# Holding seven output tiles on chip in an attention kernel, for one K slot less

## The chip, the cores and the metric

One Trainium2 chip, one core. The time is that of one launch in device microseconds; of several runs the median is taken.

## The reference

Two independent attention blocks A and B, with the same shapes and their own tensors; their outputs stand side by side in the result. Softmax is over 512 keys, everything in bfloat16.

```python
B, Sq, D = 16, 64, 640;  H, Sk, Dh = 32, 512, 128
q = (x @ wq).reshape(B, Sq, H, Dh).transpose(0, 2, 1, 3)
scores = einsum("bhqd,bhkd->bhqk", q, k_cache) * Dh ** -0.5
o = einsum("bhqk,bhkd->bhqd", softmax(scores), v_cache)
y = o.transpose(0, 2, 1, 3).reshape(B, Sq, H * Dh) @ wo
out = concatenate([y_A, y_B], axis=-1)          # 16 x 64 x 1280
```

## The kernel before

**Packs, groups, phases.** The work is cut into 128 *packs*. A pack is two batches (128 rows of queries) by four heads; it needs 1 MB of K and 1 MB of V. Four packs make a *group* (one pair of batches, 16 heads); groups are numbered 0 to 31. Eight groups make a *phase*: phase 0 is block A with heads 0 to 15, phase 1 block A with heads 16 to 31, phases 2 and 3 the same for block B. The output projection of a group is summed over its four packs in PSUM. In phases 0 and 2 the sum goes to `acc` in SBUF; in phases 1 and 3 it is added to `acc`, and the finished tile of 128 x 640 (160 KB) is stored. So there are sixteen results: groups 8 to 15 (block A) and 24 to 31 (block B). The first is stored at 230.6 us, the last at 710.7 us and, in two halves, at the end.

**What a pack does on each engine.** The names are the operations of the plan; each has an `em_` function.
- SyncE (SP) issues the loads `LDK` and `LDV`, per group `LDX` (queries), per phase `LDWQ` and `LDWO` (weights), and the stores `ST`, and `STH` for the two halves of the last result.
- TensorE: `QP` (query projection), `S` and `SL` (scores), `TR` (transposes of the probabilities), `PV` (probabilities times V), `OP` (output projection).
- VectorE (DVE): `KT` (transposes K from `kn_ring` into `kt_ring`), `RC` (reciprocals of row sums), `TE` (transposed probabilities from PSUM to `pT_sb`), `OS` (the sum of projections into `acc` or the result).
- ScalarE (ACT): `QE`, `EX` (exponential, with row sums), `OE` (product from PSUM to `oT_sb`, in two halves), `ZO` (zeros PSUM).
- GpSimd (POOL): `NM` (probabilities times reciprocal), `WP` (weights rearranged), `XS` and `XC` (transposed queries, kept in `xs_sb` for the second half of the heads).

**Order.** Nothing is scheduled at run time. `build_plan` gives each operation a due time in units of packs (pack n's scores are at time n; `AT` holds the offsets) and sorts each engine's program by it. SP's program is sorted by times of its own (`loads`): in steady state V of pack n stands at n - 2.1, K of pack m at m - 4.6, and a result's store 2.8 packs behind the start of its group's last pack. Every operation lists the resources that it reads and writes; the waits are worked out from those. Where the plan does not count an operation for the engine that has to wait, `stand_in` puts a later or equivalent operation in its place: SP's loads of K wait for `SL` of the pack that used the slot, loads of V for `TR` of the pack after it, a store for an `RC` behind its `OS`. All loads and stores go through SP's one queue, in program order.

**Buffers.** `kn_ring` has NK = 6 slots of 1 MB (8 KB in each partition), `v_ring` NV = 4. `out_sb` is one result tile, used by all stores in turn. `xs_sb` has one slot of 1280 bytes in a partition for each of the eight pairs of batches, the size of a result; its last reader in a block is `XC` of the group whose result is then formed.

**The end.** The last two packs, 126 and 127, are *narrow*: their products use row groups of 64 and their V comes in two DMAs, one for each batch. For pack 126 the operations `TE` and `PV` still take both batches at once, into banks 4 to 7; its projection goes in two halves (`OPH`) between the steps of pack 127. Pack 127 goes by halves throughout (`TRH`, `TEH` and `TEX`, `PVH`, `OEH`, `OPH`, `OSH`, `STH`). Beside it a test of all row sums runs: `FL1` on VectorE, `FLM` (a 1 x 1 matmul) on TensorE between the two `OPH` of pack 127, and `FLC`, which writes a flag. Every engine reads the flag at the end, and goes through a second, general plan only where a row sum is out of bounds; it doesn't with these inputs. TensorE runs packs 0 to 127 in a loop of four packs; what follows the `OP` of pack 125 stands behind the loop.

Of the kernel before, what the change touches and what calls it, by code (L numbers as in the profile page):

```python
# [20 lines left out]
class Cfg:  # L21
    NK = 6
    NV = 4
# [9 lines left out]
    KSPLIT = 8  # L33
    NARROW = 2
    AFTER = 24
    AT = dict(XT=-2.585, XE=-2.383, XS=-1.65, XC=-0.788, QP=-0.428, QE=-0.224, KT=(-0.672, -0.39), SL=0.1, S=0,
# [3 lines left out]
              TRH=(1.0, 1.05), TEH=(1.15, 1.2), TEX=1.2, PVH=(1.45, 1.46), OEH=(1.5, 1.55), OPY=(1.1, 1.57),  # L40
              OPZ=(1.65, 1.7), OSH=(1.75, 1.8), STH=(1.85, 1.9), FL1=1.3, FLM=1.68, FLC=1.82, WP0=(-1.6, -1.59, -0.7, -0.69, 0.25, 0.26, 1.25, 1.26),
              WP1=(-3.5, -2.55, -2.45, -1.5, -0.5, 0.5, 0.6, 1.5))
# [44 lines left out]
def build_plan(dims, cfg, general):  # L87
# [18 lines left out]
    def add_output(n):  # L106
        g, j = n // NJ, n % NJ
        final = n >= 0 and dims["FINAL"](g // NBP)
        apart = 0 <= n < cfg.KSPLIT or n >= N - cfg.NARROW
        for b in range(0 if apart else 1, 2):  # L110
            tv = n + AT["PV"]
            op = add("sp", "LDV", (n, b), tv - 0.3, [],
                     [("v" if n >= 0 else "absent", n % cfg.NV, i) for i in ((b,) if apart else (0, 1))])
            loads.append((n - cfg.NV + AT["PV"] + 0.2 if n >= 0 else -99.0, 3, op))
        if n == N - 1:
            for a in range(2):
                add("pe", "TRH", a, n + AT["TRH"][a], [("pn", n % cfg.NPN, i) for i in (2 * a, 2 * a + 1)] + [("ident",)],
                    [("SB", 2), ("SB", 3)] if a == 0 else [("SB", 0), ("SB", 1)])
                add("pe", "PVH", a, n + AT["PVH"][a], [("pT", 0, a), ("pT", 1, a)] + [("v", n % cfg.NV, b) for b in range(2)],
                    [("B", 4), ("B", 5)] if a == 0 else [("SB", 2), ("SB", 3)])  # L120
                add("act", "OEH", (n, a), n + AT["OEH"][a], [],
                    [("B", 4), ("B", 5), ("xe", 0)] if a == 0 else [("SB", 2), ("SB", 3), ("xe", 1)])
                add("pe", "OPH", (n, a), n + AT["OPZ"][a], [("xe", 0), ("xe", 1), ("wo", j)], [("B", 6 + a)])
                add("dve", "OSH", (g, a), n + AT["OSH"][a], [("acc", g % NBP)], [("B", 6 + a), ("out_sb", a)])
                loads.append((n + AT["STH"][a], 5,
                              add("sp", "STH", (g, a), n + AT["STH"][a], [("out_sb", a)], [("out_dram", g, a)])))
            add("dve", "TEH", 0, n + AT["TEH"][0], [], [("SB", 2), ("SB", 3), ("pT", 0, 0), ("pT", 1, 0)])
            add("dve", "TEH", 1, n + AT["TEH"][1], [], [("SB", 0), ("pT", 0, 1)])
            add("act", "TEX", 0, n + AT["TEX"], [], [("SB", 1), ("pT", 1, 1)])
            return  # L130
        if n > -2:
            add("pe", "TR", n, n + AT["TR"], [("pn", n % cfg.NPN, i) for i in range(4)] + [("ident",)],
                [("B", 4), ("B", 5)])
        add("dve", "TE", n, n + AT["TE"], [], [("B", 4), ("B", 5)] + [("pT", b, a) for b in range(2) for a in range(2)])
        add("pe", "PV", n, n + AT["PV"], [("pT", b, a) for b in range(2) for a in range(2)] + [("v", n % cfg.NV, 0), ("v", n % cfg.NV, 1)],
            [("B", 4), ("B", 5), ("B", 6), ("B", 7)])
        add("act", "OE", (n, 0), n + AT["OE"][0], [], [("B", 4), ("B", 5), ("oT", 0)])
        if n == N - 2:
            add("act", "OEH", (n, 1), n + AT["OE"][1], [], [("B", 6), ("B", 7), ("oT", 1)])
            for s in range(2):  # L140
                add("pe", "OPH", (n, s), n + 1 + AT["OPY"][s], [("oT", 0), ("oT", 1), ("wo", j)], [("B", 6 + s)])
            return
        add("act", "OE", (n, 1), n + AT["OE"][1], [], [("B", 6), ("B", 7), ("oT", 1)])
        add("act", "ZO", n, n + AT["ZO"], [("zeros",)], [("B", 6), ("B", 7)])
        add("pe", "OP", n, n + AT["OP"], [("oT", 0), ("oT", 1), ("wo", j)], [("B", 6), ("B", 7)])
        if j == NJ - 1:
            bp = g % NBP
            add("dve", "OS", g, n + AT["OS"], [("acc", bp)], [("B", 6), ("B", 7)]
                + ([("out_sb", 0), ("out_sb", 1)] if final else [("acc", bp)]))
            if final:  # L150
                loads.append((n + AT["ST"], 5, add("sp", "ST", g, n + AT["ST"], [("out_sb", s) for s in range(2)], [("out_dram", g)])))

    if not general:
        add("pool", "INIT1", 0, -10.0, [], [("out_sb", s) for s in range(2)])
        add("pool", "INIT2", 0, -9.9, [("out_sb", s) for s in range(2)], [("ident",)])
    for g in range(N // NJ + 1):
# [7 lines left out]
        if first:  # L164
            add("pool", "XS", g, n0 + AT["XS"], [("xe", 0), ("xe", 1)], [("xs", g % NBP)])
            if g:
                loads.append((txt - 4.05, 0, add("sp", "LDX", g, txt - 0.5, [], [("xn", g % cfg.NXN)])))
            else:
                add("act", "LDX", g, -21.0, [], [("xn", g % cfg.NXN)])
        add("pool", "XC", g, n0 + AT["XC"], [("xe", 0), ("xe", 1)] if first else [("xs", g % NBP)], [("xT", g % cfg.NX)])  # L170
    for ph in range(NPH):
# [93 lines left out]

    own = {"XC", "QE", "KT", "NM", "TE", "OE", "ZO", "OS", "LDV"}

# [13 lines left out]
    def stand_in(d, op):  # L281
# [29 lines left out]
        if d.kind == "OS":  # L311
            return at[("PV", d.idx * NJ + NJ)]
        if d.kind == "TE":
            return at[("PV", d.idx)]
# [190 lines left out]
def mha_kernel(nc, blocks, out, cfg=None):  # L505
# [26 lines left out]
    with contextlib.ExitStack() as es:  # L532
# [19 lines left out]
        zeros = sb("zeros", [128, 1], BF16)  # L552
        out_sb = sb("out_sb", [128, D], BF16)
        acc = sb("acc", [128, NBP, D], F32)
# [20 lines left out]
        def pack_info(n):  # L575
            g, j = n // NJ, n % NJ
            ph = g // NBP
            return ph // NSUB, g % NBP, j, ph % NSUB * HPH + 4 * j

        def em_INIT1(e, op):  # L580
            ins = e.memset(out_sb[:, 0:128], 1.0)
            return ins, ins

        def em_INIT2(e, op):
            ins = e.affine_select(ident[:, :], out_sb[:, 0:128], [[1, 128]], ALU.is_equal, 0.0, base=0,
                                  channel_multiplier=-1)
            return ins, ins
# [254 lines left out]
        def em_OSH(e, op):  # L842
            g, s = op.idx
            cols = slice(s * NH0, (s + 1) * NH0)
            ins = e.tensor_tensor(out_sb[:, cols], acc[:, g % NBP, cols], out_ps[:, s, :], ALU.add)
            return ins, ins

        def em_STH(e, op):
            (g, s), blk, bp = op.idx, op.idx[0] // NBP // NSUB, op.idx[0] % NBP
            cols = slice(s * NH0, (s + 1) * NH0)  # L850
            dst = out[2 * bp:2 * bp + 2, :, blk * D:(blk + 1) * D].rearrange("b q n -> (b q) n")
            ins = e.dma_start(dst[:, cols], out_sb[:, cols])
            return ins, ins

        def em_TE(e, op):
            dst = pT_sb[:, :].rearrange("p b t q -> p (b t q)")
            if op.idx == -2:
                ins = e.memset(dst, 0.0)
                return ins, ins
            ins = e.tensor_copy(dst, ps[:, 4:6, :].rearrange("p b c -> p (b c)").bitcast(BF16))  # L860
            return ins, ins

        def em_PV(e, op):
            n = op.idx
            tall, tiles, per = (32, 4, 16) if wide(n) else (64, 2, 8)
            first = last = None
            for a in range(4 // tiles):
                for b in range(2):
                    for t in range(per):
                        for s in range(tiles):  # L870
                            rows = slice(tall * s, tall * s + tall)
                            i, c = a * tiles + s, a * per + t
                            last = e.matmul(ps[:, 4 + i, 64 * b:64 * b + 64], v_ring[rows, n % NV, b, c, :],  # L873
                                            pT_sb[rows, b, c, :], start=(t == 0 and i < 2), stop=(t == per - 1),
# [4 lines left out]
        def em_OE(e, op):  # L879
            a = op.idx[1]  # L880
            ins = e.activation(oT_sb[:, 2 * a:2 * a + 2, :], o_ps[:, 2 * a:2 * a + 2, :], ACTF.Copy)  # L881
            return ins, ins
# [15 lines left out]
        def em_OS(e, op):  # L898
# [5 lines left out]
            else:  # L904
                dst = out_sb[:, :].rearrange("p (s c) -> p s c", s=2) if sub == NSUB - 1 else part
                ins = e.tensor_tensor(dst, part, out_ps, ALU.add)
            return ins, ins

        def em_ST(e, op):
            blk, bp = op.idx // NBP // NSUB, op.idx % NBP  # L910
            dst = out[2 * bp:2 * bp + 2, :, blk * D:(blk + 1) * D].rearrange("b q n -> (b q) n")
            ins = e.dma_start(dst, out_sb[:, :])
            return ins, ins
# [163 lines left out]
```

## Time and profile before

| | |
|---|---|
| time, median of 3 runs | 731.28 us (731.04 to 732.07) |
| the profiled execution: time, span | 730.47 us, 728.7 us |
| mean granted TensorE clock | 0.991 |
| busy: TensorE, VectorE, ScalarE, GpSimd | 92%, 70%, 73%, 57% of the span |
| moved by DMA | 295.02 MB, 405 GB/s over the span |
| of that written | 2.62 MB |

The span runs from the first to the last recorded instruction; the execution's time has a little around it. In a row of the timeline the first number is the start in us, the second the duration; in the chain of waits a piece named "DMA" runs from a transfer's issue to its landing, and "issue" is time in which an engine waited for nothing that the profile shows. L873 is line 873 of the listing above.

### The profile page before, as it was taken

The page shows a single profiled execution, that of the slowest core. Times are in us where ns is not written, and L with a number is a line of the kernel's source. Part 1 is how long each engine was busy: PE and PEld are TensorE (multiplying, and loading weights), DVE is VectorE, ACT ScalarE, POOL GpSimd, SP SyncE. Part 2 cuts the span into 40 slices and gives each one's busy share as a digit, 9 for nine tenths or more (in the row PEclk, how much of TensorE's full clock was granted, in tenths as well). Part 3 has the DMA queues.
Part 4 walks back from the last instruction along what each step waited for, and adds up shares of the span by engine and source line. Part 5 has one row for each costly group of instructions (what it writes and reads, how often), then busy time and mean ns, then how long its engine had stood idle before and what let it go on. Part 6 is the DMA issues. An engine that isn't in the chain of part 4 may idle for free.

```text
span 728.7 us, 61194 instructions
## 1 busy us (share of the span) xinstructions
PE 673.8 (92%) x28502; PEld 528.6 (73%) x28502; DVE 513.5 (70%) x690; ACT 533.0 (73%) x1574; POOL 417.5 (57%) x596
## 2 busy tenths in 40 slices
PE   2779999999999999999997899999999789999998
PEld 1457878778777777777776677777777568787775
DVE  6347777777777776776775667676777577778776
ACT  1448887878877777777776677767778677878785
POOL 4535656566875455554883555465587445555652
PEclk9889999999999999999999999999999999999999
DMA  8999999999999999999999999999999999999994
GB/s 338 400 406 414 414 416 413 414 416 415 412 402 411 418 416 415 417 415 417 415 410 399 417 413 413 415 413 414 415 416 405 405 415 418 416 417 418 416 416 158
DMA packets 72336, 295.02 MB, mean 405 GB/s; under 512 B 7664, under 2 KB 20080, under 8 KB 55920
## 3 DMA queue, kind: packets, MB, share of 16 engines
q1 hardware_dynamic: 72160, 294.52, 100.3%
q8 instruction: 10, 0.16, 0.1%
q10 hardware_dynamic: 144, 0.16, 0.1%
q14 instruction: 22, 0.18, 0.1%
HBM read 292.03 MB, written 2.62 MB: 404 GB/s over the span
## 4 chain that ended last, share of the span: by engine, by line
PE 54%; DMA 27%; SPq 8%; POOL 4%; DVE 3%; issue 2%; ACT 1%; DVEq 0%
PE ps L873 13%; PE ps L893 12%; DMA kn_ring<-in_B_k_cache_dram 12%; PE ps L688 11%; PE ps L718 10%; DMA kn_ring<-in_A_k_cache_dram 7%; PE ps L780 7%; DMA v_ring<-in_B_v_cache_dram 5%; SPq L631 4%; POOL pn_ring L768 3%; DMA v_ring<-in_A_v_cache_dram 3%; SPq L615 2%; DVE pT_sb L860 1%; DMA ws_sb<-in_A_wq_dram 1%; DVE kt_ring L703 1%
## 5 line engine op out<-in xcount | busy, mean ns | idle before, releaser
L768 POOL TENSOR_SCALAR pn_ring<-pn_ring,recip 128x512 bf16<-128x512 bf16 x508 | 343.0, 694 | 255.3 <-DVE recip L760 254.6
L703 DVE STREAM_TRANSPOSE kt_ring<-kn_ring 128x1024 f32<-128x1024 f32 x256 | 311.9, 1230 | 117.9 <-DMA kn_ring<-in_B_k_cache_dram 79.7
L747 ACT ACTIVATE pn_ring<-ps 128x512 bf16<-128x512 f32 x512 | 296.4, 592 | 6.3 <-PE ps L718 6.3
L860 DVE COPY pT_sb<-ps 128x2048 bf16<-128x2048 bf16 x128 | 154.2, 1205 | 48.1 <-PE ps L780 47.6
L873 PE MATMUL ps<-pT_sb,v_ring 32*128 32x64 bf16 x16448 | 160.7, 192 | 19.6 <-DMA v_ring<-in_B_v_cache_dram 8.2
L688 PE MATMUL ps<-xT_ring,wqp_sb 128*128 128x128 bf16 x2560 | 165.8, 220 | 11.2 <-POOL xT_ring L677 11.2
L873 PEld LDWEIGHTS ps<-pT_sb,v_ring 32*128 32x128 bf16 x16448 | 145.7, 91 | 34.3 <-DMA v_ring<-in_B_v_cache_dram 15.2
L688 PEld LDWEIGHTS ps<-xT_ring,wqp_sb 128*128 128x128 bf16 x2560 | 157.5, 114 | 17.5 <-issue 11.5
L893 PE MATMUL ps<-wo_sb,oT_sb 128*128 128x320 bf16 x1024 | 163.1, 303 | 0.0
L881 ACT ACTIVATE oT_sb<-ps 128x256 bf16<-128x256 f32 x257 | 84.7, 381 | 104.4 <-PE ps L873 104.4
L718 PE MATMUL ps<-kt_ring,qs_ring 32*64 32x512 bf16 x4096 | 139.1, 381 | 4.5 <-issue 4.5
L694 ACT ACTIVATE qs_ring<-ps 128x512 bf16<-128x512 f32 x128 | 76.4, 597 | 71.2 <-PE ps L688 68.9
L780 PEld LDWEIGHTS ps<-ident,pn_ring 64*128 64x128 bf16 x4096 | 68.4, 95 | 68.0 <-ACT oT_sb L881 43.4
L893 PEld LDWEIGHTS ps<-wo_sb,oT_sb 128*128 128x128 bf16 x1024 | 90.3, 98 | 36.7
L747 ACT ACTIVATION_READ_ACCUMULATOR pn_ring<-ps 128x1 f32 x512 | 105.3, 206 | 0.0
L780 PE MATMUL ps<-ident,pn_ring 64*128 64x64 bf16 x4096 | 83.0, 191 | 13.5 <-POOL pn_ring L768 7.5
L718 PEld LDWEIGHTS ps<-kt_ring,qs_ring 32*64 32x64 bf16 x4096 | 53.0, 103 | 33.3 <-issue 5.7
L760 DVE RECIPROCAL recip<-rowsum 128x2 f32<-128x2 f32 x256 | 38.4, 156 | 42.2 <-ACT pn_ring L747 40.6
L885 ACT ACTIVATE ps<-zeros 128x256 f32<-128x256 bf16 x128 | 49.5, 387 | 4.1
L656 POOL COPY wqp_sb<-ws_sb 128x1280 bf16<-128x1280 bf16 x32 | 39.6, 1255 | 9.2 <-DMA ws_sb<-in_A_wq_dram 6.5
L668 ACT ACTIVATE xe_sb<-ps 128x640 bf16<-128x640 bf16 x32 | 23.0, 717 | 3.2 <-PE ps L662 3.1
L677 POOL COPY xT_ring<-xe_sb 128x640 bf16<-128x640 bf16 x16 | 11.5, 718 | 16.7 <-PE ps L780 16.7
(42 smaller groups left out, 103.3 us busy)
## 6 DMA issues: line engine op xcount, KB each, us to landing
kn_ring<-in_B_k_cache_dram SPq DMA_DIRECT2D x128, 512.0 KB, 16.5
v_ring<-in_B_v_cache_dram SPq DMA_DIRECT2D x62, 1024.0 KB, 16.8
kn_ring<-in_A_k_cache_dram SPq DMA_DIRECT2D x112, 512.0 KB, 13.2
v_ring<-in_A_v_cache_dram SPq DMA_DIRECT2D x56, 1024.0 KB, 14.6
kn_ring<-in_A_k_cache_dram SPq DMA_DIRECT2D x32, 256.0 KB, 9.8
v_ring<-in_A_v_cache_dram SPq DMA_DIRECT2D x16, 512.0 KB, 10.4
ws_sb<-in_A_wq_dram SPq DMA_DIRECT2D x10, 512.0 KB, 9.6
wo_sb<-in_A_wo_dram SPq DMA_DIRECT2D x8, 640.0 KB, 12.7
```

Of the source, the lines that this page charges most:

```text
L688: last = e.matmul(ps[:, 1, f * 128:(f + 1) * 128], w[:, kt, f, :], xT_ring[:, xs, kt, :], start=(kt == 0), stop=(kt == KT - 1))
L694: ins = e.activation(qs_ring[:, op.idx % NQ].rearrange("p f b q -> p (f b q)"), ps[:, 1, :], ACTF.Copy, scale=scale)
L703: ins = e.transpose(dst.rearrange("p t b (h l) -> p t h b l", h=8, l=2), src)
L718: last = e.matmul(ps[64 * b:64 * b + 64, i, :], qs_ring[rows, n % NQ, f, b, :], kt_ring[rows, n % NKT, :, f // 2, b, :, f % 2], start=(f = ...
L747: ins = e.activation(dst, src, ACTF.Exp, scale=1.0, accum_out=sum_of(h))
L768: ins = e.tensor_scalar(pn_view(h), pn_view(h), recip[:, h:h + 1], 1.0, ALU.mult, ALU.mult)
L780: last = e.transpose(pt_bank(b)[:, 64 * c:64 * c + 64], pn[rows, c, :], ident[rows, rows], tile_position=(64 * b, 0))
L860: ins = e.tensor_copy(dst, ps[:, 4:6, :].rearrange("p b c -> p (b c)").bitcast(BF16))
L873: last = e.matmul(ps[:, 4 + i, 64 * b:64 * b + 64], v_ring[rows, n % NV, b, c, :], pT_sb[rows, b, c, :], start=(t == 0 and i < 2), stop=(t ...
L881: ins = e.activation(oT_sb[:, 2 * a:2 * a + 2, :], o_ps[:, 2 * a:2 * a + 2, :], ACTF.Copy)
L885: ins = e.activation(z_ps, zeros[:, :].unsqueeze(2).broadcast_to([128, 2, 128]), ACTF.Copy)
L893: last = e.matmul(out_ps[:, s, :], oT_sb[:, i, :], wo_sb[:, 4 * j + i, s * NH0:(s + 1) * NH0], start=(j == 0 and i == 0), stop=(j == NJ - ...
```

## The change

- **Results.** `out_sb` becomes seven tiles (NHOLD = 7). The results of groups 8 to 14 stay in them. The other results, group 15 and all of block B, are written into the `xs_sb` slot of their pair of batches.
- **Stores.** The stores of groups 8 to 14, and those of groups 24 and 25 (LATE), move in SP's program to 125.95, behind the last V (at 124.9) and the store of group 30 (at 125.8), ahead of the two `STH`.
- **K ring.** NK goes from 6 to 5: 8 KB in each partition less, for 7.5 KB more of `out_sb`.
- **Pack 126.** `TE` and `PV` go by batches: `TE` and `PV` for the first, the new `TEB` and `PVB` for the second. The first two of the four products go to banks 0 and 1, columns 256 to 383, where the last scores stood, and `OE` takes them from there. The transposes `TRH` 1 of pack 127 write other columns of these banks, and by the plan's resources wait for that `OE`.
- **Flag.** `FLM` moves from 1.68 to 1.72, behind the second `OPH` of pack 127 (1.7).

```diff
-    NK = 6
+    NK = 5
...
+    NHOLD = 7
+    LATE = (24, 25)
+    LATEST = -2.05
...
-              ... FL1=1.3, FLM=1.68, FLC=1.82, ...
+              ... FL1=1.3, FLM=1.72, FLC=1.82, ...
...
+        held = g < N // NJ // 2 and g % NBP < cfg.NHOLD
+        result = [("held", g % NBP, s) if held else ("xs", g % NBP, s) for s in range(2)]
...
+        if n == N - 2:
+            for b in range(2):
+                add("dve", ("TE", "TEB")[b], n, n + AT["TE"] + 0.01 * b, [], [("B", 4 + b), ("pT", b, 0), ("pT", b, 1)])
+                add("pe", ("PV", "PVB")[b], n, n + AT["PV"] + 0.01 * b, [("pT", b, 0), ("pT", b, 1), ("v", n % cfg.NV, b)],
+                    [("SB", 0), ("SB", 1), ("B", 6), ("B", 7)])
+            add("act", "OE", (n, 0), n + AT["OE"][0], [], [("SB", 0), ("SB", 1), ("oT", 0)])
+            add("act", "OEH", (n, 1), n + AT["OE"][1], [], [("B", 6), ("B", 7), ("oT", 1)])
...
             if final:
-                loads.append((n + AT["ST"], 5, add("sp", "ST", g, n + AT["ST"], [("out_sb", s) for s in range(2)], [("out_dram", g)])))
+                late = held or g in cfg.LATE
+                loads.append((N + cfg.LATEST + 0.001 * g if late else n + AT["ST"], 5,
+                              add("sp", "ST", g, N + cfg.LATEST + 0.001 * g if late else n + AT["ST"], result, [("out_dram", g)])))
...
-        out_sb = sb("out_sb", [128, D], BF16)
+        out_sb = sb("out_sb", [128, cfg.NHOLD, D], BF16)
...
+        def result(g):
+            if g // NBP < NSUB and g % NBP < cfg.NHOLD:
+                return out_sb[:, g % NBP]
+            return xs_sb[:, g % NBP, 0:D]
...
         def em_TE(e, op):
             dst = pT_sb[:, :].rearrange("p b t q -> p (b t q)")
+            if op.idx == NPACK - 2:
+                ins = e.tensor_copy(pT_sb[:, 0].rearrange("p t q -> p (t q)"), pt_bank(0))
+                return ins, ins
...
+        def o_bank(n, i):
+            return ps[:, i, 256:384] if n == NPACK - 2 and i < 2 else ps[:, 4 + i, 0:128]
...
         def em_ST(e, op):
...
-            ins = e.dma_start(dst, out_sb[:, :])
+            ins = e.dma_start(dst, result(op.idx))
```

More of the change, by code (lines that the diff above doesn't have):

```diff
@@ L40 @@
               TRH=(1.0, 1.05), TEH=(1.15, 1.2), TEX=1.2, PVH=(1.45, 1.46), OEH=(1.5, 1.55), OPY=(1.1, 1.57),
-              OPZ=(1.65, 1.7), OSH=(1.75, 1.8), STH=(1.85, 1.9), FL1=1.3, FLM=1.68, FLC=1.82, WP0=(-1.6, -1.59, -0.7, -0.69, 0.25, 0.26, 1.25, 1.26),
+              OPZ=(1.65, 1.7), OSH=(1.75, 1.8), STH=(1.85, 1.9), FL1=1.3, FLM=1.72, FLC=1.82, WP0=(-1.6, -1.59, -0.7, -0.69, 0.25, 0.26, 1.25, 1.26),
               WP1=(-3.5, -2.55, -2.45, -1.5, -0.5, 0.5, 0.6, 1.5))
@@ L123, in add_output @@
                 add("pe", "OPH", (n, a), n + AT["OPZ"][a], [("xe", 0), ("xe", 1), ("wo", j)], [("B", 6 + a)])
-                add("dve", "OSH", (g, a), n + AT["OSH"][a], [("acc", g % NBP)], [("B", 6 + a), ("out_sb", a)])
+                add("dve", "OSH", (g, a), n + AT["OSH"][a], [("acc", g % NBP)], [("B", 6 + a), result[a]])
                 loads.append((n + AT["STH"][a], 5,
-                              add("sp", "STH", (g, a), n + AT["STH"][a], [("out_sb", a)], [("out_dram", g, a)])))
+                              add("sp", "STH", (g, a), n + AT["STH"][a], [result[a]], [("out_dram", g, a)])))
             add("dve", "TEH", 0, n + AT["TEH"][0], [], [("SB", 2), ("SB", 3), ("pT", 0, 0), ("pT", 1, 0)])
@@ L133, in add_output @@
                 [("B", 4), ("B", 5)])
+        if n == N - 2:
[5 more added lines that the diff above has]
+            add("act", "OEH", (n, 1), n + AT["OE"][1], [], [("B", 6), ("B", 7), ("oT", 1)])
+            for s in range(2):
+                add("pe", "OPH", (n, s), n + 1 + AT["OPY"][s], [("oT", 0), ("oT", 1), ("wo", j)], [("B", 6 + s)])
+            return
         add("dve", "TE", n, n + AT["TE"], [], [("B", 4), ("B", 5)] + [("pT", b, a) for b in range(2) for a in range(2)])
@@ L137, in add_output @@
         add("act", "OE", (n, 0), n + AT["OE"][0], [], [("B", 4), ("B", 5), ("oT", 0)])
[L138 to L142, printed above, removed]
         add("act", "OE", (n, 1), n + AT["OE"][1], [], [("B", 6), ("B", 7), ("oT", 1)])
@@ L148, in add_output @@
             add("dve", "OS", g, n + AT["OS"], [("acc", bp)], [("B", 6), ("B", 7)]
-                + ([("out_sb", 0), ("out_sb", 1)] if final else [("acc", bp)]))
+                + (result if final else [("acc", bp)]))
             if final:
-                loads.append((n + AT["ST"], 5, add("sp", "ST", g, n + AT["ST"], [("out_sb", s) for s in range(2)], [("out_dram", g)])))
+                late = held or g in cfg.LATE
+                loads.append((N + cfg.LATEST + 0.001 * g if late else n + AT["ST"], 5,
+                              add("sp", "ST", g, N + cfg.LATEST + 0.001 * g if late else n + AT["ST"], result, [("out_dram", g)])))
     if not general:
-        add("pool", "INIT1", 0, -10.0, [], [("out_sb", s) for s in range(2)])
-        add("pool", "INIT2", 0, -9.9, [("out_sb", s) for s in range(2)], [("ident",)])
+        add("pool", "INIT1", 0, -10.0, [], [("held", 0, s) for s in range(2)])
+        add("pool", "INIT2", 0, -9.9, [("held", 0, s) for s in range(2)], [("ident",)])
     for g in range(N // NJ + 1):
@@ L164, in build_plan @@
         if first:
-            add("pool", "XS", g, n0 + AT["XS"], [("xe", 0), ("xe", 1)], [("xs", g % NBP)])
+            add("pool", "XS", g, n0 + AT["XS"], [("xe", 0), ("xe", 1)], [("xs", g % NBP, s) for s in range(2)])
             if g:
@@ L169, in build_plan @@
                 add("act", "LDX", g, -21.0, [], [("xn", g % cfg.NXN)])
-        add("pool", "XC", g, n0 + AT["XC"], [("xe", 0), ("xe", 1)] if first else [("xs", g % NBP)], [("xT", g % cfg.NX)])
+        add("pool", "XC", g, n0 + AT["XC"], [("xe", 0), ("xe", 1)] if first else [("xs", g % NBP, s) for s in range(2)], [("xT", g % cfg.NX)])
     for ph in range(NPH):
@@ L264, in build_plan @@
             op.deps = [d for d in op.deps if d.kind != "WP"]
-    own = {"XC", "QE", "KT", "NM", "TE", "OE", "ZO", "OS", "LDV"}
+    own = {"XC", "QE", "KT", "NM", "TE", "TEB", "OE", "ZO", "OS", "LDV"}
     def for_pe(d):
@@ L312, in stand_in @@
             return at[("PV", d.idx * NJ + NJ)]
+        if d.kind == "TEB":
+            return at[("PVB", d.idx)]
         if d.kind == "TE":
@@ L578, in pack_info @@
             return ph // NSUB, g % NBP, j, ph % NSUB * HPH + 4 * j
+        def result(g):
+            if g // NBP < NSUB and g % NBP < cfg.NHOLD:
+                return out_sb[:, g % NBP]
+            return xs_sb[:, g % NBP, 0:D]
         def em_INIT1(e, op):
-            ins = e.memset(out_sb[:, 0:128], 1.0)
+            ins = e.memset(out_sb[:, 0, 0:128], 1.0)
             return ins, ins
         def em_INIT2(e, op):
-            ins = e.affine_select(ident[:, :], out_sb[:, 0:128], [[1, 128]], ALU.is_equal, 0.0, base=0,
+            ins = e.affine_select(ident[:, :], out_sb[:, 0, 0:128], [[1, 128]], ALU.is_equal, 0.0, base=0,
                                   channel_multiplier=-1)
@@ L844, in em_OSH @@
             cols = slice(s * NH0, (s + 1) * NH0)
-            ins = e.tensor_tensor(out_sb[:, cols], acc[:, g % NBP, cols], out_ps[:, s, :], ALU.add)
+            ins = e.tensor_tensor(result(g)[:, cols], acc[:, g % NBP, cols], out_ps[:, s, :], ALU.add)
             return ins, ins
@@ L851, in em_STH @@
             dst = out[2 * bp:2 * bp + 2, :, blk * D:(blk + 1) * D].rearrange("b q n -> (b q) n")
-            ins = e.dma_start(dst[:, cols], out_sb[:, cols])
+            ins = e.dma_start(dst[:, cols], result(g)[:, cols])
             return ins, ins
@@ L861, in em_TE, with em_TEB, em_PVB, product @@
             return ins, ins
+        def em_TEB(e, op):
+            ins = e.tensor_copy(pT_sb[:, 1].rearrange("p t q -> p (t q)"), pt_bank(1))
+            return ins, ins
         def em_PV(e, op):
-            n = op.idx
+            return product(e, op.idx, (0,) if op.idx == NPACK - 2 else (0, 1))
+        def em_PVB(e, op):
+            return product(e, op.idx, (1,))
+        def o_bank(n, i):
+            return ps[:, i, 256:384] if n == NPACK - 2 and i < 2 else ps[:, 4 + i, 0:128]
+        def product(e, n, halves):
             tall, tiles, per = (32, 4, 16) if wide(n) else (64, 2, 8)
@@ L867, in em_PV @@
             for a in range(4 // tiles):
-                for b in range(2):
+                for b in halves:
                     for t in range(per):
@@ L872, in em_PV @@
                             i, c = a * tiles + s, a * per + t
-                            last = e.matmul(ps[:, 4 + i, 64 * b:64 * b + 64], v_ring[rows, n % NV, b, c, :],
+                            last = e.matmul(o_bank(n, i)[:, 64 * b:64 * b + 64], v_ring[rows, n % NV, b, c, :],
                                             pT_sb[rows, b, c, :], start=(t == 0 and i < 2), stop=(t == per - 1),
@@ L880, in em_OE @@
             a = op.idx[1]
-            ins = e.activation(oT_sb[:, 2 * a:2 * a + 2, :], o_ps[:, 2 * a:2 * a + 2, :], ACTF.Copy)
+            src = ps[:, 0:2, 256:384] if op.idx == (NPACK - 2, 0) else o_ps[:, 2 * a:2 * a + 2, :]
+            ins = e.activation(oT_sb[:, 2 * a:2 * a + 2, :], src, ACTF.Copy)
             return ins, ins
@@ L904, in em_OS @@
             else:
-                dst = out_sb[:, :].rearrange("p (s c) -> p s c", s=2) if sub == NSUB - 1 else part
+                dst = result(g).rearrange("p (s c) -> p s c", s=2) if sub == NSUB - 1 else part
                 ins = e.tensor_tensor(dst, part, out_ps, ALU.add)
```

## The prediction

> **What bounds the kernel now.** I read the profile page first (busy tenths and DMA row), then the busy time by windows, the chain of waits in order of time, the queue of SyncE (SP) and the timeline of the last 12 us.
>
> ```profile
> span 728.7 us, 61194 instructions
> DMA  8999999999999999999999999999999999999994
> 100.00:150.00 50.00, 50.00 (x2200) 39.39 (x2199) 38.94 (x52) 40.39 (x120) 29.87 (x45) 1.00 1.02 415
> 400.00:450.00 50.00, 45.02 (x1968) 35.38 (x1969) 33.23 (x47) 35.35 (x105) 27.09 (x40) 1.00 1.02 415
> 550.00:600.00 50.00, 43.54 (x1895) 33.70 (x1882) 31.91 (x44) 34.76 (x103) 28.60 (x40) 1.00 1.03 408
> 600.00:650.00 50.00, 50.00 (x2144) 40.02 (x2145) 39.41 (x53) 40.28 (x120) 27.32 (x41) 1.00 1.02 417
> 650.00:700.00 50.00, 50.00 (x2137) 39.36 (x2124) 38.62 (x51) 40.22 (x121) 27.85 (x42) 1.00 1.02 417
> 577.10 17.51 DMA kn_ring<-in_B_k_cache_dram
> 594.64 1.25 DVE kt_ring L703
> 597.16 2.71 POOL pn_ring L768 x4
> 600.64 1.19 PE ps L893 x8
> ```
>
> The window rows give the stretch, PE busy, PEld, DVE, ACT, POOL, then granted clock, DMA share and GB/s. The DMA engines are full in every stretch, and they move 415 to 417 GB/s where the loads are K and V. TensorE is full too at 100 to 150 us and from 600 us on (50.00 of 50), but between them it idles: 45.02 and 43.54 of 50. So two resources of nearly equal price take turns. In the middle each pack waits for its bytes; the last wait of that sort in the chain is the K load that lands at 594.6 us and releases DVE's transpose, the normalisation and TensorE. From there to the last pack the chain is TensorE without a gap. Whatever is taken out of the transfer stream before 594.6 us therefore starts that last TensorE run earlier by the time of those bytes. What is taken out later gives TensorE nothing, since it no longer waits.
>
> **The seven held stores.**
>
> ```profile
> L912 SPq DMA_DIRECT2D out_dram<-out_sb x15: 368/594/1692, 230.6 to 710.7; - x15
> out_dram<-out_sb SPq DMA_DIRECT2D x15, 160.0 KB, 17.1
> wo_sb<-in_B_wo_dram SPq DMA_DIRECT2D x8, 640.0 KB, 15.8
> ```
>
> The first store is issued at 230.6 us. Results 8 to 14 (seven of the first block's eight) come every four packs from there, all far before 594.6 us and all in the DMA-bound middle. One store is 160 KB = 163,840 B; at 417 GB/s that is 0.39 us. The upper price comes from the window at 550 us, where four of the 640 KB output-weight loads, with rows as short as a store's, fall: 408 for 417 GB/s is 9 x 50 us = 0.45 MB or 1.08 us lost on 16 store sizes, 0.07 us each, so 0.46 us. I take 0.40, nearer to the first, because the windows from 600 us hold stores as well and still show 417. Seven give **2.8 us** (2.75 to 3.2), and TensorE had idle time enough to use it: 5 us in the window at 400 us alone. The stores' places in SP's queue cost nothing when vacated; the loads behind them were waiting for TensorE, not for SP.
>
> **Five K slots instead of six.**
>
> ```profile
> 691.58 1.07 PE L718 MATMUL ps<-kt_ring,qs_ring 32*64 32x512 bf16 x32
> 692.59 0.64 PE L780 MATMUL ps<-ident,pn_ring 64*128 64x64 bf16 x32
> 693.26 0.37 SPq L641 DMA_DIRECT2D v_ring<-in_B_v_cache_dram  x1
> 693.68 3.30 SPq L631 DMA_DIRECT2D kn_ring<-in_B_k_cache_dram  x2
> DMA to landing us min/median/max: 14.9/15.8/18.2
> ```
>
> These are, in order, the scores of pack 122, the transposes of pack 121, then SP's issue of V of pack 124 and of K of pack 127; the last row is the K loads' time from issue to landing from 650 us on. SP's list puts K of pack m right behind V of pack m-3, and that V waits for the transposes of pack m-6 (V has four slots): V leaves just as they end. A ring of five makes K of pack m wait for the scores of pack m-5, which stand ahead of those same transposes in TensorE's program. So the new condition has always been met when SP gets there; the sixth slot was never the one that gated. At the start the same order holds, as V of pack 2 already waits for a transpose behind pack 0's scores. Cost 0; if I have the order wrong by a pack, K leaves 5 us later, and the cover is the queue itself: 15.8 us from issue to landing, nearly all of it waiting behind other loads, so the engines would not run dry.
>
> **Where the nine stores go, and the two of the second block.**
>
> ```profile
> 690.30 0.68 SPq L912 DMA_DIRECT2D out_dram<-out_sb  x1
> 710.72 1.08 SPq L912 DMA_DIRECT2D out_dram<-out_sb  x1
> 726.08 1.00 SPq L852 DMA_DIRECT2D out_dram<-out_sb  x2
> 716.00:720.30 4.30, 4.01 (x210) 2.79 (x207) 2.39 (x4) 3.68 (x11) 1.79 (x3) 1.00 0.34 130
> 720.30:728.70 8.40, 5.55 (x177) 3.81 (x172) 4.75 (x15) 2.33 (x7) 0.00 (x0) 1.00 0.10 28
> ```
>
> The first two rows are the stores of results 29 and 30, 20.4 us apart. Counted back at that pace, results 24 and 25 are stored at about 588 and 609 us: they queue behind the last K that is waited for. Moving them spares the transfers 0.8 us and TensorE nothing.
>
> SP issues all nine behind the store of result 30, so at about 711.8 - 2.8 = 709 us, at 0.59 us each (median above) some 5.3 us: done by 714.5. The last two half stores then come at 726.08 - 2.8 = 723.3 us. Queued ahead of these are only the late stores. The total of bytes is unchanged and the engines never pause, so the stream runs dry where it does now, at about 720.3 us: 3 us before the final stores need it. Cost 0, cover 3 us. The last V lands ahead of the stores, 9 x 0.40 = 3.6 us earlier than now, while its user moves by 2.8.
>
> **Pack 126 by batches, and the flag's matmul.**
>
> ```profile
> 717.04 1.07 PE L718 MATMUL ps<-kt_ring,qs_ring 32*64 32x512 bf16 x32
> 718.61 1.26 PE L893 MATMUL ps<-wo_sb,oT_sb 128*128 128x320 bf16 x8
> 718.79 1.23 DVE L860 COPY pT_sb<-ps 128x2048 bf16<-128x2048 bf16 x1 [1.88 <-PE ps L780]
> 721.54 0.69 DVE L803 COPY pT_sb<-ps 128x1024 bf16<-128x1024 bf16 x1
> 721.31 0.38 ACT L881 ACTIVATE oT_sb<-ps 128x256 bf16<-128x256 f32 x1 [0.71 <-PE ps L873]
> 720.16 1.11 PE L873 MATMUL ps<-pT_sb,v_ring 64*128 64x64 bf16 x64 [0.29 <-DVE pT_sb L860]
> 721.09 0.84 PE L791 MATMUL ps<-ident,pn_ring 64*128 64x64 bf16 x32
> 722.02 0.72 PE L837 MATMUL ps<-wo_sb,oT_sb 128*128 128x320 bf16 x4
> 722.67 0.58 PE L818 MATMUL ps<-pT_sb,v_ring 64*128 64x64 bf16 x28
> 723.50 0.77 PE L818 MATMUL ps<-pT_sb,v_ring 64*128 64x64 bf16 x36 [0.24 <-issue]
> 725.46 0.10 PE ps L929
> ```
>
> The first two rows are the last pack's scores and the last projection of TensorE's loop, which ends at 719.87. The copy of 1.23 us becomes two of 0.69 us (the row of that shape). The first half of the product can begin 0.54 us earlier and the whole ends about 0.4 us earlier, so the copy to oT_sb does too. What follows does not gain: the second half of pack 127's transposes needs the normalisations, which stand behind the copies on DVE and now come up to 2 x 0.69 - 1.23 = 0.15 us later. The new wait, of those transposes for the copy out of banks 0 and 1 (0.38 us, over by about 721.3 - 2.8), ends before the normalisations do; queued behind it on TensorE is the rest of the tail. The 0.15 us in turn lies under the gap at 723.50, "issue": 28 of the 64 matmuls of the last product run, then TensorE stands for 0.24 us. Cost 0; without that gap it would be up to 0.15. The flag's matmul stands between the two output projections; behind them, it gives back its **0.10 us** of the chain. Its own result is then later by one projection, hidden behind the final addition on DVE and the landing of the last store.
>
> **What the gap at 723.50 is.**
>
> ```profile
> 31.05 1.49 PE L718 MATMUL ps<-kt_ring,qs_ring 32*64 32x512 bf16 x19 [4.54 <-issue]
> 43.51 0.72 PE L780 MATMUL ps<-ident,pn_ring 64*128 64x64 bf16 x20 [3.79 <-issue]
> q8 instruction: 1, 0.02, 13.4%
> q8 instruction: 1, 0.02, 27.4%
> ```
>
> The last two rows are the DMA queues of 28.5 to 29.0 us and of 721.0 to 721.25 us: one instruction packet of 16 KB each, 2.1 to 2.5 us before TensorE goes on (31.05 and 723.50). So TensorE's program is fetched in pieces. At the start, with full engines, the piece costs 4.54 and 3.79 us of standing. At the end, where the loop has been left and the DMA engines run dry, 0.24. With the late stores the engines are busier when TensorE leaves its loop (about 717 us instead of 719.9): at that absolute time the row from 716 us shows a share of 0.34. I charge **+0.2 us**, between 0 (the piece's engine is free) and about 2.0 (it waits until the stream is dry at 720.3, and TensorE goes on 2.4 us later at 722.7, not at 723.5 - 2.8 = 720.7).
>
> [...]
>
> **Sum.** -2.8 - 0.1 + 0.2 = -2.7 us. The profiled execution took 730.47 us (span 728.7), 0.8 under the median of 731.28. So it would read 727.8, and the median 731.28 - 2.7 = **728.6 us**. A difference under about 0.2% (1.5 us) can't be told from none.
>
> **Rivals.**
>
> *The fetch waits for the stores* (0.18). The mechanism of the gap, at its upper end: 0.9 to 2.0 us more in the tail, gain 2.9 - 2.0 = 0.9 to 2.0, times 729.3 to 730.4. For it: 4.54 and 3.79 us under full engines. Against: a share of only 0.34. Half of it is faster by over 0.2%, half within.
>
> *The transfers were hidden anyway* (0.06). TensorE full at 100 to 150 and from 600 us on speaks for it; 45.02 of 50 and the K wait up to 594.6 us speak against it. Only 0.1 us for the flag remains: 731.2.
>
> *The late stores don't stream* (0.07): slower.
>
> ```profile
> out_dram<-out_sb SPq DMA_DIRECT2D x2, 80.0 KB, 1.6
> ```
>
> If each pays the 1.6 us of a lone store in series, ten (result 30 with them) take 16 us from about 714 us, when most engines are through with V, to 730. The final halves land 1.6 us later at 731.6, and the span ends some 3 us beyond 728.7: median about 734. It decides from (723.3 - 714) / 10 = 0.9 us a store on. Against it: stores in mid-stream leave 417 GB/s untouched. [...]
>
> *All nine count* (0.03): TensorE also uses the two later stores; 3.6 + 0.1, 727.6.
>
> **Numbers.** The forecast holds 0.66, 728.6 with 728.0 to 729.2 as its own range. Faster by over 0.2%: 0.66 + 0.09 + 0.03 = 0.78; within: 0.09 + 0.06 = 0.15; slower: 0.07. The range goes from 727.6 (all nine, or 0.46 us a store) to 730.5 (fetch at its worst); outside lie the hidden case and the slower one.
>
> **What would show it.** The last K wait of the chain ends near 591.9 instead of 594.64, and the last pack's scores start near 714.2 instead of 717.04: the main step. The last product's gap stays near 0.24 us; 1 us or more there is the first rival. The output projections of pack 127 stand back to back. SP shows no new wait ahead of K loads, and issue to landing stays near 16 us; less than about 10 would say that five slots starve the queue. The late stores land before the final halves are issued. If the scores come 2.8 us earlier and the end does not, the tail is to blame; if they don't, the middle was not bound by bytes.

## The result and the profile after

| | before | changed |
|---|---|---|
| median of 5 runs | 731.04 us | 727.95 us |
| ratio, 95% interval | | 0.9958 [0.9946, 0.9969] |
| profiled execution: time, span | 730.47, 728.7 us | 727.84, 726.1 us |

The change makes the kernel 3.1 us faster by the medians, 2.6 us by the two profiled spans; 2.7 us was forecast. Here are the rows of the changed kernel that answer to those shown of before: span and DMA row of the page, busy time by windows (us, PE busy, PEld, DVE, ACT, POOL, clock, DMA share, GB/s), the last K wait in the chain, and the DMA issues of the stores (KB, us to landing).

```profile
span 726.1 us, 61183 instructions
DMA  8999999999999999999999999999999999999996
100.00:150.00 50.00, 50.00 (x2202) 39.42 (x2201) 38.80 (x52) 40.32 (x120) 29.94 (x45) 1.00 1.02 415
400.00:450.00 50.00, 44.83 (x1851) 35.45 (x1854) 34.39 (x48) 36.94 (x109) 25.85 (x39) 1.00 1.02 415
650.00:700.00 50.00, 50.00 (x2174) 39.75 (x2171) 38.77 (x52) 39.44 (x118) 29.05 (x43) 1.00 1.02 417
```
```profile
577.86 19.11 DMA kn_ring<-in_B_k_cache_dram
596.99 1.25 DVE kt_ring L722
599.50 2.70 POOL pn_ring L787 x4
602.98 1.19 PE ps L928 x8
```
```profile
out_dram<-xs_sb SPq DMA_DIRECT2D x8, 160.0 KB, 14.1
out_dram<-out_sb SPq DMA_DIRECT2D x7, 160.0 KB, 6.1
out_dram<-xs_sb SPq DMA_DIRECT2D x2, 80.0 KB, 1.6
```

The kernel is the same kind of thing as before: transfers full to the end, TensorE full at both ends and idling in the middle. Where the time went is seen best in the start of each pack's scores, taken from the two timelines:

| scores of pack | 33 | 41 | 49 | 59 | 69 | 89 | 103 | 115 | 127 |
|---|---|---|---|---|---|---|---|---|---|
| changed minus before, us | +0.15 | -0.60 | -1.50 | -1.99 | -2.59 | -2.47 | -2.94 | -2.87 | -2.52 |

Nothing moves in the first quarter. Behind the first vacated store (230.6 us before, at pack 38) the scores come earlier and earlier, by 2.6 us at pack 69, and from there on the saving stays at about that (2.5 to 2.9 us in the table). So the gain is made in the middle, and carried to the end. The entries at packs 41 and 49 alone would not show it: the run with five slots below, with every store in place, is 0.9 and 0.8 us ahead there too, but only 0.1 us at packs 69 and 89.

The tail, TensorE's rows behind the last scores:

```profile
714.52 1.07 PE L737 MATMUL ps<-kt_ring,qs_ring 32*64 32x512 bf16 x32
717.29 1.11 PE L907 MATMUL ps<-pT_sb,v_ring 64*128 64x64 bf16 x64
718.44 0.41 PE L810 MATMUL ps<-ident,pn_ring 64*128 64x64 bf16 x16
719.16 0.41 PE L810 MATMUL ps<-ident,pn_ring 64*128 64x64 bf16 x16 [0.32 <-DVE pn_ring L787]
721.06 0.77 PE L837 MATMUL ps<-pT_sb,v_ring 64*128 64x64 bf16 x37 [0.33 <-issue]
722.32 1.25 PE L856 MATMUL ps<-wo_sb,xe_sb 128*128 128x320 bf16 x8
```

Pack 126's product starts 2.77 us behind the last scores where it was 3.12, but the second half of the transposes waits for the normalisations (0.32, DVE), and the last product has its gap as before (0.33 us of "issue" for 0.24). The two projections stand back to back. From the last scores to the end of the span it is 11.6 us, and was 11.7.

### The profile page after: what moved, and what is told of

It is laid out like the page before. It is cut to its first block, busy times and chain, and to the rows that moved or that the text cites. A ratio compares the mean times of both kernels' runs of the same rounds, so it can differ in the third digit from the quotient of the medians.

```text
span 726.1 us, 61183 instructions
## 1 busy us (share of the span) xinstructions
PE 675.0 (93%) x28502; PEld 530.5 (73%) x28502; DVE 514.9 (71%) x691; ACT 533.1 (73%) x1574; POOL 416.1 (57%) x596
## 4 chain that ended last, share of the span: by engine, by line
PE 62%; DMA 24%; SPq 6%; DVE 3%; POOL 3%; issue 2%; ACT 1%; DVEq 0%
PE ps L907 14%; PE ps L928 14%; PE ps L707 13%; DMA kn_ring<-in_B_k_cache_dram 12%; PE ps L737 12%; PE ps L799 7%; DMA kn_ring<-in_A_k_cache_dram 5%; DMA v_ring<-in_B_v_cache_dram 5%; SPq L650 3%; POOL pn_ring L787 2%; DMA ws_sb<-in_A_wq_dram 1%; DVE kt_ring L722 1%; DVE pT_sb L882 1%; SPq L634 1%; SPq L640 1%
## 5 line engine op out<-in xcount | busy, mean ns | idle before, releaser
L907 PE MATMUL ps<-pT_sb,v_ring 32*128 32x64 bf16 x16448 | 162.6, 192 | 16.1 <-DMA v_ring<-in_B_v_cache_dram 7.3
L707 PEld LDWEIGHTS ps<-xT_ring,wqp_sb 128*128 128x128 bf16 x2560 | 157.5, 114 | 17.6 <-issue 11.6
L907 PEld LDWEIGHTS ps<-pT_sb,v_ring 32*128 32x128 bf16 x16448 | 146.8, 91 | 31.4 <-DMA v_ring<-in_B_v_cache_dram 14.6
## 6 DMA issues: line engine op xcount, KB each, us to landing
v_ring<-in_B_v_cache_dram SPq DMA_DIRECT2D x62, 1024.0 KB, 16.7
v_ring<-in_A_v_cache_dram SPq DMA_DIRECT2D x56, 1024.0 KB, 14.9
```

The costliest lines, as they stand in the source:

```text
L707: last = e.matmul(ps[:, 1, f * 128:(f + 1) * 128], w[:, kt, f, :], xT_ring[:, xs, kt, :], start=(kt == 0), stop=(kt == KT - 1))
L907: last = e.matmul(o_bank(n, i)[:, 64 * b:64 * b + 64], v_ring[rows, n % NV, b, c, :], pT_sb[rows, b, c, :], start=(t == 0 and i < 2), stop ...
```

## The experiments

The theory, "bytes": the gain is the transfer time of seven stores, taken out of the stream ahead of the last K wait; the smaller K ring, pack 126 and the late stores cost nothing. Rivals: the ring costs something; the gain comes from buffers or from SP's waits; it is made in the tail. Each run below was timed beside the kernel before on its own chip. Times are written "this run to before", both medians; then comes their ratio with its 95% interval.

**Five slots alone.** `-NK = 6` `+NK = 5` in the kernel before.

> The kernel before with NK = 5 and nothing else. Theory 'bytes' (the gain is the transfer time of the stores that leave the stream ahead of the last K wait; the sixth K slot never gated a load): same time as before, within 0.3 us, the K loads' time from issue to landing unchanged at 15 to 17 us. Rival 'slots' (the smaller ring costs something, which the held stores more than pay back): slower by 0.5 us or more, with SP waiting ahead of K loads and landings under 14 us.

731.20 to 731.03 us, 1.0002 [0.9993, 1.0011]; the K loads from 650 us on landed after 14.6/16.3/18.4 us (minimum, median, maximum; 14.9/15.8/18.2 before). SP's waits name the same instructions as before and no new one ahead of K. No load had been waiting for the sixth slot.

**Stores in place.**

> The changed kernel with every store at its old place in SP's program: seven tiles, five slots, pack 126 by batches and the flag's matmul last stay. Theory 'bytes': the whole main gain is gone; before less 0.1 us for the flag (about 0.999 to 1.001 of before). Rival 'buffers' (the gain comes from results having tiles of their own, so that no sum waits for an older store to land): the time of the changed kernel, 2.7 to 3.1 us under before.

```diff
-                late = held or g in cfg.LATE
+                late = False
```

730.41 to 731.03 us, 0.9992 [0.9983, 1.0001]. By the interval, tiles of their own for the results bring about 1.2 us at most, and "buffers" needed 2.7 to 3.1. It falls: the places of the stores make the main gain.

**The seven stores alone, and a surprise.**

> The changed kernel with only the seven stores of the first block late (results 24 and 25 in place), pack 126 whole and the flag's matmul between the projections, as before. Theory 'bytes': 7 x 0.39 = 2.7 us under before, and the scores of packs 70 to 100 2.6 to 2.8 us earlier. Rival 'tail' (a good part of the gain is made behind the last scores): 2.2 us or less under before.

```diff
-    LATE = (24, 25)
+    LATE = ()
...
-... FLM=1.72 ...
+... FLM=1.68 ...
...
-        if n == N - 2:
-            for b in range(2):
-                add("dve", ("TE", "TEB")[b], ...
...
```

731.67 to 731.03 us, 1.0009 [1.0000, 1.0018]: no gain at all, though the scores of pack 127 began at 714.91 us, 2.1 us earlier than before, and the last addition ended at 724.84 (before: 726.73). The time was lost behind it. These are the rows of the barrier at the end, where each engine stops until all have come (all five go on at 730.0 to 730.1 us), by engine queue, with duration in ns and start in us, and SP's wait for it:

```profile
L541 ACTq DRAIN  x1: 64/64/64, 725.9 to 725.9; - x1
L541 PEldq DRAIN  x1: 62/62/62, 726.0 to 726.0; - x1
L541 SPq DRAIN  x1: 13/13/13, 726.6 to 726.6; - x1
L541 DVEq DRAIN  x1: 53/53/53, 729.9 to 729.9; - x1
```
```profile
SPq L541 <- PEq L541: 3.5, 1, 3.5
```

VectorE takes its closing branch on the flag at 725.89 us, and gets to the barrier at 729.9, 3.9 us behind TensorE and 3.3 behind SP, the last of the others. (The wait is put down to TensorE's queue; its drain was long done, and VectorE's was not.) No operation of VectorE is left there, so the reading is that it lacks program. The trace has two DMA queues of kind "instruction", q8 and q14, with 10 and 22 packets over the changed kernel's run; they are read here as pieces of the engines' programs. These are their packets up to the closing branch, first with the seven stores alone, 716 to 726 us, then in the changed kernel, 714 to 724 us:

```profile
q8 instruction: 2, 0.03, 1.2%
```
```profile
q8 instruction: 2, 0.03, 1.3%
q14 instruction: 1, 0.01, 0.2%
```

One packet of queue q14 is missing. It is not lost but late: these are the packets from 725 to 731 us, first with the seven stores alone, then with the same kernel and one instruction more (the run e3b below):

```profile
q14 instruction: 5, 0.04, 2.2%
```
```profile
q14 instruction: 4, 0.03, 2.0%
```

Over the whole run both have 22 in q14. Four of the five come at 726.5 to 726.9 us, while VectorE stands, and one at 730.5, when it has gone on; in the other kernel all four come at 726.6 to 727.0, with VectorE already at the barrier. By the count, the packet that the second kernel has ahead of the branch comes behind it in the first. The programs as built tell why it may be: in the kernel before, each result's sum also waits for an older store, and a second wait is written as an instruction of its own (EVENT_SEMAPHORE in the traces: VectorE has 24 of them before, 9 in the changed kernel). With tiles of their own fifteen such waits go away, and the second copy of pack 126 comes in, so VectorE reads the flag at its instruction 702 in the changed kernel, instead of 716. Pack 126 whole has one copy less: 701.

**Pack 126 whole, and the same with one instruction more.** The first is the changed kernel without the split; the second adds to it one memset of an unused tile, which brings VectorE back to 702. The next run does the same with the seven stores alone.

> The changed kernel with pack 126's copies and product whole again; all nine stores stay late, the flag's matmul stays last. VectorE's program up to the end is one instruction shorter than the changed kernel's (no second copy). Theory 'code layout' (the missing gain of the run with the seven stores alone is an instruction fetch of VectorE at the closing branch, which comes with that length): about 3.7 us slower than the changed kernel, 0.5 to 1 us slower than the kernel before, with VectorE's last drain some 4 us behind the other engines'. Rival 'batches' (the late stores hold up the whole product of pack 126, and going by batches is what avoids it): the same time, but then pack 126's product or what follows it starts later behind the scores than in the changed kernel by 3 us.

> The kernel with pack 126 whole, with one instruction added to VectorE's program: a memset of an unused tile of 128 x 1 at the start. Theory 'code layout': the 3.7 us are gone; the time of the changed kernel within 0.3 us (ratio to before 0.995 to 0.997). Rival 'batches': nothing changes, still slower than before.

> The seven stores alone (results 24 and 25 in place, pack 126 whole, flag's matmul between the projections), with the same added memset. Theory 'bytes' with 'code layout': 2.2 to 2.8 us under before, so nearly the whole gain of the change. Rival 'batches': no faster than before.

```diff
+        pad = sb("pad", [128, 1], F32)
...
         def em_WZ(e, op):
+            e.memset(pad[:, :], 0.0)
```

| | flag read at | median, before | ratio, 95% interval | VectorE's drain |
|---|---|---|---|---|
| pack 126 whole | 701 | 731.50, 731.10 us | 1.0008 [0.9999, 1.0017] | 729.8 us |
| the same, one more | 702 | 728.40, 731.10 us | 0.9964 [0.9951, 0.9978] | 726.3 us |
| seven alone | 701 | 731.67, 731.03 us | 1.0009 [1.0000, 1.0018] | 729.9 us |
| the same, one more | 702 | 728.69, 731.10 us | 0.9967 [0.9955, 0.9979] | 726.2 us |

A memset that does nothing is worth 3 us, twice. Both pairs show the q14 packet ahead of the branch with 702 and none with 701. So "batches" falls, and the seven stores alone give 2.4 us of the 3.1. Going by batches itself is worth less than these intervals resolve (0.9958 and 0.9964); that it lengthens VectorE's program by one is what the changed kernel needs of it. That the late packet is what VectorE stood for is read from the packets and the drain; at which instruction a piece ends was not tried further.

**Results 24 and 25 in place.**

> The changed kernel with results 24 and 25 stored at their old places. Theory 'bytes': within 0.3 us of the changed kernel, since TensorE no longer waits for transfers behind pack 105. Rival 'all nine count': 0.4 to 0.8 us slower than the changed kernel, so 2.3 us or less under before.

727.88 to 731.03 us, 0.9961 [0.9948, 0.9975]: as the changed kernel. The interval, 1.8 to 3.8 us under before, does not shut out the rival's 2.3. The traces side with "bytes": the last pack's scores come 2.01 us earlier than before, and 2.04 in the changed kernel when it was run again.

**Stored twice.**

> The changed kernel, with the seven held results stored twice: at their old places and again behind the last V (the same values to the same place). Theory 'bytes': 7 x 0.39 = 2.7 us slower than the changed kernel, 0.1 to 0.6 us under before, the same as with the stores in place only, so the seven late stores cost the tail nothing. Rival 'queue' (the gain came from SP's waits, not from bytes, or the late stores cost the tail): differs from the run with the stores in place by 0.5 us or more.

```diff
+                if held:
+                    loads.append((n + AT["ST"], 5, add("sp", "STX", g, n + AT["ST"], result, [("out_dram", g)])))
...
```

730.64 to 731.10 us, 0.9993 [0.9984, 1.0002]. Beside the changed kernel, seven stores put back into the middle cost 0.9993 - 0.9958 = 0.0035 of 731, 2.6 us, known to about 1 us. Beside the stores in place (0.9992), the late stores at the end cost nothing measurable. This is the cleanest test of the main step: one edit, the same tail, and the gain is gone. It puts back the stores' turns in SP's program with their bytes, so it can't tell these two apart. The trace of before can: SP waited at none of the seven stores, while the DMA engines were full all the time (share 1.02 from 225 to 375 us) and a K load took 16.7 us in the median from issue to landing.

**The flag's matmul between.**

> The changed kernel with the flag's matmul back between the two output projections. Theory: 0.1 us slower than the changed kernel, by one matmul of 0.10 us in the chain; the intervals can't tell that apart, the chain of the tail can. Rival 'the flag decides': its result is later behind the projections, so putting it back is 0.2 us or more faster.

728.38 to 731.20 us, 0.9960 [0.9946, 0.9974]: not told apart, as expected. The chain has the matmul at its price:

```profile
722.16 1.19 PE ps L856 x8
723.35 0.10 PE ps L964
723.45 0.66 PE ps L856 x4
```

**Thirteen late stores.** `-LATE = (24, 25)` `+LATE = (24, 25, 26, 27, 28, 29)`.

> The changed kernel with results 26 to 29 late as well: thirteen stores behind the last V instead of nine. Theory 'bytes': TensorE gains nothing in its last run (no transfer is waited for behind pack 105). SP issues a late store about every 1.03 us from 708 us on, so thirteen end near 722.5 us, still ahead of the final halves at 723.6: the changed kernel's time within 0.4 us. Rival 'stores don't stream': the final halves are issued 1 us or more later and land behind a queue, 1 to 3 us slower than the changed kernel.

727.10 to 731.20 us, 0.9945 [0.9931, 0.9958]. No slower; SP's last late store was out by 719.8 us and the final halves went out at 723.43. The scores of pack 127 even began at 713.83 us, 3.2 us before those of the kernel before. Both kernels were run once more, side by side.

> The changed kernel itself, on the same chip as the next run: 0.995 to 0.997 of before.

> Thirteen late stores once more, beside the changed kernel. Theory 'stores in the last stretch lengthen some of TensorE's products by about 0.13 us each' (none is longer than 1.24 us without them): the last pack's scores 0.6 to 0.7 us earlier than in the changed kernel, of which the instruction fetch behind the late stores takes back about 0.5 us; 0 to 0.9 us faster than the changed kernel. Rival 'scatter of a run': no difference, and the scores' time differs by less than 0.3 us.

728.05 and 727.37 us to 730.99; 0.9958 [0.9944, 0.9971] and 0.9946 [0.9932, 0.9959]. The order of the medians is the same in both sets, 0.7 to 0.9 us apart, but the intervals overlap, and only the second set was run on one chip. In the profiled execution of thirteen late stores the second time, the slowest of its five, the last scores came at 715.17 us, not earlier than in its neighbour (715.00), so that part of the expectation failed; it had come 1.1 us later than its neighbour out of the middle. Between packs 100 and 127, though, thirteen late stores gain on the kernel before by 0.71 and 0.67 us in the two runs, nine lose 0.14 (in the first) and 0.23 (in the second, from 2.27 to 2.04 us ahead). The products of packs 113, 117 and 118 show it, first of the changed kernel, then with thirteen late:

```profile
651.46 1.36 PE L907 MATMUL ps<-pT_sb,v_ring 32*128 32x64 bf16 x128
672.13 1.36 PE L907 MATMUL ps<-pT_sb,v_ring 32*128 32x64 bf16 x128
677.30 1.39 PE L907 MATMUL ps<-pT_sb,v_ring 32*128 32x64 bf16 x128
```
```profile
651.47 1.22 PE L907 MATMUL ps<-pT_sb,v_ring 32*128 32x64 bf16 x128
671.87 1.22 PE L907 MATMUL ps<-pT_sb,v_ring 32*128 32x64 bf16 x128
676.90 1.22 PE L907 MATMUL ps<-pT_sb,v_ring 32*128 32x64 bf16 x128
```

Between 604 and 707 us the changed kernel has five products of 1.34 to 1.39 us, the two runs with thirteen late stores have none over 1.24, and each of the twelve profiled kernels with stores in that stretch has five or six over 1.24. Each of the changed kernel's five holds a pause: a matmul begins 0.09 to 0.18 us behind the one before it, where the longest step in the products of the other is 0.03. What makes the pause is not shown. It is not tied to stores alone: the kernel before has such products at 192, 213 and 218 us already, ahead of its first store, while output weights are loaded, and none from 100 to 190 us. Thirteen late stores have the best medians measured, though not clear of the changed kernel's by the intervals.

## Why the prediction was right

- **The seven stores, -2.8 us:** right in mechanism and place, and in size within what the runs resolve: 2.59 us by pack 69, 2.6 us put back by storing twice.
- **Five slots, 0:** right (1.0002).
- **The two of the second block, 0:** right for two, within the intervals. But "gives TensorE nothing" looks too strong: without any store in its last run the medians are 0.7 to 0.9 us lower, in two pairs whose intervals overlap, and the products lose their pauses. The chain showed no gap, because a pause of 0.1 to 0.2 us inside a product is not a row of its own there. That it is a wait for transfers is not shown.
- **The late stores in the tail, 0:** right, with a cover smaller than worked out. SP took 1.03 us for a store, not 0.59:

```profile
708.69 7.24 SPq L947 DMA_DIRECT2D out_dram<-out_sb  x7
715.97 2.38 SPq L947 DMA_DIRECT2D out_dram<-xs_sb  x2
723.58 0.87 SPq L871 DMA_DIRECT2D out_dram<-xs_sb  x2
```

  They were out at 718.35 us, not 714.5, and the final halves still found SP free for 5.2 us. The mis-sized term is the median of 0.59: it came from stores issued far apart. 1.03 us is even over the 0.9 us from which the prediction let "the late stores don't stream" decide; the stores had begun at 708.7 us and not at 714, and that left the room. The rival falls by the thirteen as well.
- **The fetch, +0.2 us (0 to 2.0):** inside its bounds, but no run shows the 0.2 itself (the gap went from 0.24 to 0.33 us in the changed kernel), nor that the fetch waits for the stores. Without late stores the gap is 0.24 us (before), 0.65 (five slots alone) and none (stores in place). With late stores it is 0.05 in three runs, 0.32 in two, then 0.33, 0.48, 0.65, 0.66, 0.87 and 1.02. The two ranges overlap almost whole. These are the ends of it with late stores, the changed kernel again and pack 126 whole with one more:

```profile
721.22 0.05 issue
720.95 1.02 issue
```

  The second reaches the 1 us that the prediction named as the sign of its first rival, once in eleven runs; that kernel was still 2.7 us under before. No run here tells how long the piece stood behind the stores, if it did.
- **Pack 126, 0:** right as a number, and in part by luck. The prediction weighed only what the split adds to the work. It left out that results in tiles of their own drop fifteen waits from VectorE's program, which puts its end one instruction from a stall of 3.9 us. The split's second copy happened to be that instruction. With pack 126 whole the forecast of -2.7 us would have been wrong by all of it (1.0008).
- **The flag, -0.1:** right in the chain; too small for the times to show.
- **What would show it:** the last pack's scores began at 714.52 us, 714.2 was named. The last K wait did not end near 591.9 but at 596.99 us. The chain shows it for the next pack (105 instead of 104), whose scores are 3.25 us earlier; as a sign for the main step that row was badly chosen, the scores' starts are the better one.

## What to carry to other kernels

Here transfers and TensorE cost nearly the same (from 400 to 450 us of the changed kernel the DMA share is 1.02 and TensorE is busy for 44.83 of 50 us), and a transfer's price depended on where it stood. Seven stores ahead of the last wait for data cost their bytes over the rate, about 2.6 us, and nothing measurable in the tail, where the DMA share is down to 0.07 from 720 to 722 us (0.9993 stored twice, 0.9992 with the stores in place). Find that last wait in the chain, and move what nobody waits for behind it. And when a run shows no gain though the work ends earlier, look at the last microseconds by engine queue: here a branch at the end cost 3.0 us, more than the 2.4 us that the seven stores brought, and one instruction more or less decided it.

## What the runs showed of the hardware

When VectorE's program was one instruction shorter, it reached the barrier 4.0 us behind its closing branch instead of 0.6, and the launch took 3.0 to 3.1 us longer. Four runs agree, two with the instruction and two without, and the instruction packets beside them: one ahead of the branch with it, that one behind the branch without. Which target the branch took, and why the shorter program has that packet late, no trace here shows. TensorE's gaps look alike: in the thirteen runs that have one in the last product, TensorE goes on 2.2 to 2.8 us after the start of an instruction packet of queue q8 (2.4 before: 721.09 to 723.50; 2.5 in the changed kernel: 718.57 to 721.06).

Some of TensorE's groups of matmuls held a pause of 0.09 to 0.18 us that no view of waits lists. They were found by comparing the lengths of equal groups: 1.22 us without, 1.34 to 1.39 with one.
